# One score tile of two PSUM banks, with one maximum, scaling, sum and reciprocal per tile of tokens

## The chip, the core and the metric

One core of one Trainium2 chip. The metric is the device time of one execution in microseconds, lower is better. TensorE (PE) multiplies, VectorE (DVE) and ScalarE (ACT) work element by element, GpSimd (POOL) does one product per half tile, and SyncE (SP) issues all DMAs. Each engine runs its instructions in the order in which they stand in its queue.

## The reference

```python
def _attn_ref(q, k, v):                       # (4, 8, 576, 64): batch, heads, tokens, head size
    scores = scale * np.matmul(q, k.transpose(0, 1, 3, 2))
    rel = pos[:, None] - pos[None, :]
    scores = np.where((rel >= 0) & (rel < 64), scores, -1000000000.0)
    scores = scores - np.max(scores, axis=-1, keepdims=True)
    attn = np.exp(scores)
    attn = attn / (np.sum(attn, axis=-1, keepdims=True) + 1e-09)
    return np.matmul(attn, v)

def _moe_ref(x, w_in, w_out, g_ln):           # x (2304, 512), w_in (512, 1024), w_out (1024, 512)
    h = x @ w_in
    e = np.exp(h - np.max(h, axis=-1, keepdims=True))
    solu = h * (e / (np.sum(e, axis=-1, keepdims=True) + 1e-09))
    ln = (solu - mean(solu)) / np.sqrt(var(solu) + 1e-06) * g_ln
    return ln @ w_out

def _moe2_ref(x, w_in, w_out, a, b):          # w_in (512, 2048), w_out (2048, 512)
    h = x @ w_in
    g = (a[0] + a[1]*h + a[2]*h**2 + a[3]*h**3) / (1 + abs(b[0])*abs(h) + abs(b[1])*h**2 + 1e-06)
    return g @ w_out
```

The output is `_moe2_ref(_moe_ref(attention))` over 2304 tokens.

## The kernel before

The 2304 tokens are 18 tiles of 128. A first stage carries each tile through attention and the first expert layer; a second stage does the second expert layer in 6 blocks of 384 tokens. The weights come as 64-bit floats and are converted on the chip, chunk by chunk of 512 columns. The chunks are named `i` (first layer in, 8 half chunks), `o` (first layer out, 8) and `c` (second layer, 32). For each, ACT reads the words twice, DVE does a clamp (L518), a shift (L520), a merge (L522), an add (L525) and a remainder (L313 or L540), and ACT the rounded high part. A product of two 32-bit matrices is three products of high and low parts.

One tile t passes these steps; their names stand in `step(...)`:

- `scores` (L412, L418): PE adds the mask and multiplies q by k for 8 heads. The heads lie in two PSUM tiles of one bank each, `s{t}_0` and `s{t}_1`, four heads a tile.
- `max0`, `max1` (L426, L427): for each half, DVE takes the maximum per head and scales it.
- `exp00` to `exp13` (L432): ACT takes one exponential per head, with its sum.
- `sum0`, `sum1` (L438, L439): for each half, DVE adds 1e-9 and takes the reciprocal of four sums.
- `norm0`, `norm1` (L443): POOL multiplies a half by its reciprocals.
- `probs0`, `probs1` (L449): PE transposes a half; ACT copies it out (L317).
- `attend` (L466): PE multiplies by v. `att_hi`, `att_lo` (L317, L313): high part and remainder `xh`, `xl`.
- `h0` to `h3` (L554 to L556): 24 products into `h`, two PSUM banks, of which there is one pair (ring `h` of 1).
- `solu_max` (L562), `solu_exp` (L566), `solu_mul` (L571): maximum over 1024 columns, exponential, product. `solu_mul` gives `h` back, so that the next tile's `h0` can start.
- `ln_square` to `ln_apply` (L578 to L604): the layer norm. `lnT0`, `lnT1` (L614): transposes. `ln_hi`, `ln_lo`: high part and remainder.
- Every third tile: `x2_0` to `x2_3` (L632 to L634), the output products of three tiles, which need all `o` chunks.

The order is not written out by hand. The class `Schedule` gives each step a due time (from `WANT`, `PACE` and a table `SHIFT` of one number per step), then walks through time with a duration for each step and takes on each engine the ready step that is due first. `RINGS` says how many tiles of a kind may be held at once (scores: one tile of tokens). The names `L...` are lines of the profile.

Of the kernel before, what the change touches and what calls it, by code (L numbers as in the profile page):

```python
# [10 lines left out]
F32 = mybir.dt.float32  # L11
# [4 lines left out]
AF = mybir.ActivationFunctionType  # L16
ALU = mybir.AluOpType
AX = mybir.AxisListType
# [10 lines left out]
class Schedule:  # L29
# [248 lines left out]
def attention_moe_moe2(ctx: ExitStack, tc, q, k, v, w1, w1o, g_ln, w2, w2o, num, den, out):  # L278
# [122 lines left out]
    def scores(t):  # L401
# [18 lines left out]
        for j in range(2):  # L420
            tiles["s", t, j] = s[j]

    def soft_max(t, j):
        mx, su, rc = stat[t]
        sl = slice(NPAIR * j, NPAIR * j + NPAIR)
        nc.vector.reduce_max(mx[:, sl], tiles["s", t, j], axis=AX.X, negate=True)  # L426
        nc.vector.tensor_scalar_mul(mx[:, sl], mx[:, sl], 0.125)  # L427
# [611 lines left out]
```

## Time and profile before

| | |
|---|---|
| time, median of 3 runs | 728.79 us (728.03 to 729.09) |
| the profiled execution's own time | 727.53 us |
| its span, first to last instruction | 725.8 us |
| PE busy | 691.9 us (95%) |
| DVE busy | 615.3 us (85%) |
| ACT busy | 498.6 us (69%) |
| POOL busy | 48.0 us (7%) |
| mean granted clock of PE | 0.991 |

Busy time is the union of an engine's instructions. Successive instructions of one engine can overlap by some tenths of a microsecond, so the price of one in a row of them is read from start to start. The granted clock is a share of PE's full speed: 1.00 is 2.4 GHz, 0.50 is 1.2 GHz.

### The profile page before, as it was taken

What the parts mean: (1) busy time and instruction counts of PE and PEld (TensorE: products, weight loads), DVE (VectorE), ACT (ScalarE), POOL (GpSimd) and SP (SyncE); (2) the same over time, 40 slices, a digit from 0 to 9 for tenths busy, and PEclk for the clock granted to TensorE, in tenths of its full rate; (3) what the DMA queues carried; (4) which work ended last, traced back from release to release, by engine and by line L of the source; (5) the groups of instructions that cost most, each with busy time, mean ns of one, the idle gap of its engine ahead of it and who ended that gap; (6) DMA issues with size and microseconds to landing.
All of it is one profiled execution on the core that took longest, in us unless ns stands there. A gap on an engine that the chain in (4) does not pass through costs nothing.

```text
span 725.8 us, 12000 instructions
## 1 busy us (share of the span) xinstructions
PE 691.9 (95%) x4536; PEld 617.8 (85%) x4536; DVE 615.3 (85%) x999; ACT 498.6 (69%) x986; POOL 48.0 (7%) x51
## 2 busy tenths in 40 slices
PE   2689789999999999999999999999999999999997
PEld 1567579998988989999899999899899889899986
DVE  6999988989999997777999889688878778876873
ACT  6898775777677774657776766666665658566662
POOL 3212120012111110000000000000000000000000
PEclk9999989999999999999999999999999999999999
DMA  9764445667578635506220200010020001000001
GB/s 292 281 190 132 162 148 193 209 217 249 193 222 293 204 108 201 166 20 218 80 87 12 77 1 22 35 32 0 23 66 1 22 1 45 0 1 30 15 0 44
DMA packets 47785, 77.85 MB, mean 107 GB/s; under 512 B 5040, under 2 KB 23472, under 8 KB 47728
## 3 DMA queue, kind: packets, MB, share of 16 engines
q1 hardware_dynamic: 47728, 77.09, 32.7%
q8 instruction: 36, 0.59, 0.3%
q14 instruction: 21, 0.17, 0.1%
HBM read 59.25 MB, written 17.83 MB: 106 GB/s over the span
## 4 chain that ended last, share of the span: by engine, by line
PE 90%; DVE 4%; ACT 2%; DMA 2%; issue 1%; SPq 0%; POOL 0%; POOLq 0%
PE hp L829 9%; PE hp L828 9%; PE hp L827 9%; PE o L893 9%; PE o L892 9%; PE o L891 9%; PE x L632 5%; PE x L634 5%; PE x L633 5%; PE h L554 4%; PE h L555 4%; PE h L556 4%; PE pl L614 2%; PE s L418 2%; PE pv L466 2%; PE pt L449 2%
## 5 line engine op out<-in xcount | busy, mean ns | idle before, releaser
L829 PE MATMUL hp<-x2h,w 128*128 128x384 f32 x384 | 129.5, 337 | 0.0
L827 PE MATMUL hp<-x2h,w 128*128 128x384 f32 x384 | 129.3, 337 | 0.0
L828 PE MATMUL hp<-x2l,w 128*128 128x384 f32 x384 | 129.3, 337 | 0.0
L893 PE MATMUL o<-w,gl 128*128 128x512 f32 x282 | 111.4, 395 | 0.0
L892 PE MATMUL o<-w,gh 128*128 128x512 f32 x282 | 111.0, 394 | 0.0
L891 PE MATMUL o<-w,gh 128*128 128x512 f32 x282 | 110.8, 393 | 0.0
L837 ACT ACTIVATE w<-hp,ab 128x768 f32<-128x768 f32 x48 | 43.4, 905 | 72.6 <-PE hp L829 72.6
L845 DVE SCALAR_TENSOR_TENSOR w<-r,b,w 128x768 f32<-128x768 f32 x48 | 48.8, 1017 | 38.9 <-ACT r L839 38.9
L827 PEld LDWEIGHTS hp<-x2h,w 128*128 128x128 f32 x384 | 72.1, 188 | 3.2
L828 PEld LDWEIGHTS hp<-x2l,w 128*128 128x128 f32 x384 | 72.1, 188 | 3.2
L829 PEld LDWEIGHTS hp<-x2h,w 128*128 128x128 f32 x384 | 72.1, 188 | 0.3 <-DVE w L313 0.3
L875 ACT CAST gh<-t 128x768 fp32r<-128x768 f32 x48 | 40.3, 839 | 41.9 <-PE o L892 35.3
L632 PE MATMUL x<-lh,wo 128*128 128x384 f32 x192 | 66.7, 347 | 0.0
L554 PE MATMUL h<-wi,xh 128*128 128x512 f32 x144 | 58.9, 409 | 6.6 <-ACT xh L317 3.9
L634 PE MATMUL x<-lh,wo 128*128 128x384 f32 x192 | 65.0, 339 | 0.0
L633 PE MATMUL x<-ll,wo 128*128 128x384 f32 x192 | 65.0, 338 | 0.0
L893 PEld LDWEIGHTS o<-w,gl 128*128 128x128 f32 x282 | 52.9, 188 | 12.3
L892 PEld LDWEIGHTS o<-w,gh 128*128 128x128 f32 x282 | 52.9, 188 | 9.5
L891 PEld LDWEIGHTS o<-w,gh 128*128 128x128 f32 x282 | 52.9, 188 | 9.2
L443 POOL TENSOR_TENSOR P<-P,rc 128x512 f32<-128x512 f32 x36 | 44.8, 1248 | 224.9 <-DVE rc L439 127.7
L313 DVE TENSOR_TENSOR gl<-t,gh 128x768 fp32r<-128x768 f32 x48 | 45.9, 956 | 16.1 <-ACT gh L875 16.0
L556 PE MATMUL h<-wi,xl 128*128 128x512 f32 x144 | 57.1, 397 | 2.2 <-DVE xl L313 2.2
(105 smaller groups left out, 1495.1 us busy)
## 6 DMA issues: line engine op xcount, KB each, us to landing
v<-in_v_dram SPq DMA_DIRECT2D x35, 256.0 KB, 4.6
xc<-in_moe_w_in_dram SPq DMA_DIRECT2D x16, 512.0 KB, 3.6
w2d<-Ac SPq DMA_DIRECT2D x32, 256.0 KB, 3.2
xc<-in_moe_w_out_dram SPq DMA_DIRECT2D x16, 512.0 KB, 4.1
r<-w2d SPq DMA_DIRECT2D x32, 256.0 KB, 3.3
k<-in_k_dram SPq DMA_DIRECT2D x17, 384.0 KB, 4.8
q<-in_q_dram SPq DMA_DIRECT2D x18, 256.0 KB, 3.5
x2d<-xs SPq DMA_DIRECT2D x6, 768.0 KB, 4.5
```

The lines of the kernel that those rows point to most:

```text
L554: nc.tensor.matmul(o, xh[:, c, :], wh, start=(c == 0), stop=False)
L556: nc.tensor.matmul(o, xl[:, c, :], wh, start=False, stop=(c == KC - 1))
L632: nc.tensor.matmul(o, wh, lh[:, f, :], start=(f == 0), stop=False)
L633: nc.tensor.matmul(o, wh, ll[:, f, :], start=False, stop=False)
L634: nc.tensor.matmul(o, wl, lh[:, f, :], start=False, stop=(f == FC1 - 1))
L827: nc.tensor.matmul(h, wh[:, sl], xh[:, c], start=(c == 0), stop=False)
L828: nc.tensor.matmul(h, wh[:, sl], xl[:, c], start=False, stop=False)
L829: nc.tensor.matmul(h, wl[:, sl], xh[:, c], start=False, stop=(c == KC - 1))
L845: nc.vector.scalar_tensor_tensor(out=w, in0=r, scalar=b1, in1=w, op0=ALU.mult, op1=ALU.add)
L891: nc.tensor.matmul(o, gh[:, n, sl], wh, start=(f == 0), stop=False)
L892: nc.tensor.matmul(o, gh[:, n, sl], wl, start=False, stop=False)
L893: nc.tensor.matmul(o, gl[:, n, sl], wh, start=False, stop=(f == FC2 - 1))
```

## The change

The two score tiles become one tile `s{t}` over two banks. `max0` and `max1` become `max`, `sum0` and `sum1` become `sum`. The exponentials, the products on POOL and everything behind them stay as they were, except that each waits for the joint step. Some durations by which the planner reckons are edited, and the table `SHIFT` has new numbers for nearly all steps, so the order of all engines is another one. `WANT`, `PACE`, `ALT` and `RINGS` are the same. Behind the change, lines 410 to 440 stand 3 to 6 lines higher: L426 is then L421, L438 is L432, L562 is L556, L571 is L565.

```diff
@@ -167,106 +167,102 @@
 SHIFT = {
-    "zeros.0": 13.46, "load_q.0": 28.35, "load_k.0": 44.58, "load_v0.0": 54.08, "load_v1.0": 16.74, "scores.0": 14.59,
+    "zeros.0": -29.74, "load_q.0": 8.57, "load_k.0": -32.25, "load_v0.0": 110.71, "load_v1.0": 3.99, "scores.0": 4.78,
...
-    pS = psS.enter_context(tc.tile_pool(name="pS", bufs=2, space=PSUM, side="right"))
+    pS = psS.enter_context(tc.tile_pool(name="pS", bufs=1, space=PSUM, side="right"))
...
-        s = [pS.tile([P, NPAIR, P], F32, name=f"s{t}_{j}", tag="S") for j in range(2)]
+        both = pS.tile([P, 2, NPAIR, P], F32, name=f"s{t}", tag="S")
+        s = [both[:, j] for j in range(2)]
...
-        for j in range(2):
-            tiles["s", t, j] = s[j]
-
-    def soft_max(t, j):
+        tiles["s", t] = both
+
+    def soft_max(t):
         mx, su, rc = stat[t]
-        sl = slice(NPAIR * j, NPAIR * j + NPAIR)
-        nc.vector.reduce_max(mx[:, sl], tiles["s", t, j], axis=AX.X, negate=True)
-        nc.vector.tensor_scalar_mul(mx[:, sl], mx[:, sl], 0.125)
+        nc.vector.reduce_max(mx, tiles["s", t].rearrange("p j c k -> p (j c) k"), axis=AX.X, negate=True)
+        nc.vector.tensor_scalar_mul(mx, mx, 0.125)
...
-        nc.scalar.activation(Pn[t][:, j, n, :], tiles["s", t, j][:, n, :], AF.Exp, bias=mx[:, c:c + 1], scale=0.125,
+        nc.scalar.activation(Pn[t][:, j, n, :], tiles["s", t][:, j, n, :], AF.Exp, bias=mx[:, c:c + 1], scale=0.125,
                              accum_out=su[:, c:c + 1])
 
-    def soft_sum(t, j):
+    def soft_sum(t):
         mx, su, rc = stat[t]
-        sl = slice(NPAIR * j, NPAIR * j + NPAIR)
-        nc.vector.tensor_scalar_add(rc[:, sl], su[:, sl], 1.0e-9)
-        nc.vector.reciprocal(rc[:, sl], rc[:, sl])
+        nc.vector.tensor_scalar_add(rc, su, 1.0e-9)
+        nc.vector.reciprocal(rc, rc)
...
-        step("scores", "PE", 1.2, ["load_q", "load_k", ("constants", 0), ("zeros", 0)], scores, t, want=WANT["scores"],
+        step("scores", "PE", 1.25, ["load_q", "load_k", ("constants", 0), ("zeros", 0)], scores, t, want=WANT["scores"],
              take=[("s", t), ("P", t)], give=[("q", t), ("k", t)])
+        step("max", "DVE", 1.42, ["scores"], soft_max, t)
         for j in range(2):
-            step(f"max{j}", "DVE", 0.87, ["scores"], soft_max, t, j)
             for n in range(4):
-                step(f"exp{j}{n}", "ACT", 0.36, [f"max{j}"], soft_exp, t, j, n, give=[("s", t)])
-            step(f"sum{j}", "DVE", 0.35, [f"exp{j}{n}" for n in range(4)], soft_sum, t, j)
-            step(f"norm{j}", "POOL", 1.12, [f"sum{j}"], soft_norm, t, j)
+                step(f"exp{j}{n}", "ACT", 0.36, ["max"], soft_exp, t, j, n, give=[("s", t)])
+        step("sum", "DVE", 0.37, [f"exp{j}{n}" for j in range(2) for n in range(4)], soft_sum, t)
+        for j in range(2):
+            step(f"norm{j}", "POOL", 1.12, ["sum"], soft_norm, t, j)
...
-        step("attend", "PE", 0.98, ["probs_copy0", "probs_copy1", "load_v0", "load_v1"], attend, t, want=WANT["attend"],
+        step("attend", "PE", 1.05, ["probs_copy0", "probs_copy1", "load_v0", "load_v1"], attend, t, want=WANT["attend"],
...
-            step(f"h{c}", "PE", 1.385, needs + [("cv7", "i", c, hf) for hf in range(2)], h_mm, t, c,
+            step(f"h{c}", "PE", 1.39, needs + [("cv7", "i", c, hf) for hf in range(2)], h_mm, t, c,
...
-            step(f"lnT{hf}", "PE", 0.434, ["ln_apply"] + needs + ([("lnT1", t - 1)] if t else []), ln_T, t, hf,
+            step(f"lnT{hf}", "PE", 0.45, ["ln_apply"] + needs + ([("lnT1", t - 1)] if t else []), ln_T, t, hf,
...
-                step(f"x2_{dc}", "PE", 4.2, needs + [("cv7", "o", c) for c in range(FC1)], x2_mm, pr, dc,
+                step(f"x2_{dc}", "PE", 4.25, needs + [("cv7", "o", c) for c in range(FC1)], x2_mm, pr, dc,
```

Three places show how the order moves. In the rows below the number behind a tile's letters is the tile of tokens or the weight chunk (`rc6`: reciprocals of tile 6; `wo_7`: `o` chunk 7), the last number only counts buffers.

**First pair**: DVE ahead of the fifth `solu_mul` (`e4`). Before:

```order
L588 TENSOR_SCALAR st3_1064<-st3_1064 128x1
L540 SCALAR_TENSOR_TENSOR wo_7_1167<-Ao_7_873,gT_98,wo_7_1167 128x512
L562 TENSOR_REDUCE st4_1188<-h4_1127 128x1
L540 SCALAR_TENSOR_TENSOR wo_2_1181<-Ao_2_984,gT_98,wo_2_1181 128x512
L438 TENSOR_SCALAR rc6_899<-sum6_898 128x4
L439 RECIPROCAL rc6_899<-rc6_899 128x4
L518 TENSOR_SCALAR co_5_1151<-co_5_1151 128x512
L313 TENSOR_TENSOR ll0_794<-pl2_0_1067,lh0_793 128x4x128
L571 ISA e4_1189,st4_1188<-h4_1127,e4_1189 128x1024
```

The same place of DVE now:

```order
L534 SCALAR_TENSOR_TENSOR wo_2_1151<-Ao_2_848,gT_98,wo_2_1151 128x512
L556 TENSOR_REDUCE st4_1169<-h4_1102 128x1
L309 TENSOR_TENSOR ll0_670<-pl2_1_1144,lh0_669 128x4x128
L432 TENSOR_SCALAR rc7_1031<-sum7_1030 128x8
L433 RECIPROCAL rc7_1031<-rc7_1031 128x8
L516 SCALAR_TENSOR_TENSOR co_6_1008<-xo_6_831,co_6_1008 128x512
L565 ISA e4_1170,st4_1169<-h4_1102,e4_1170 128x1024
```

Between the maximum of tile 4 and its product stood the second half sum of tile 6; now the joint sum of tile 7 stands there, and that of tile 6 some 30 rows further up.

**Second pair**: PE at the first `h` product (tile 0). Before:

```order
L466 MATMUL pv0_295<-PT0_1_288,v0_1_204 64x64
L554 MATMUL h0_352<-wi_0_0_177,xh0_293 128x512
L555 MATMUL h0_352<-wi_0_0_177,xh0_293 128x512
L556 MATMUL h0_352<-wi_0_0_177,xl0_294 128x512
L554 MATMUL h0_352<-wi_0_1_229,xh0_293 128x512
L555 MATMUL h0_352<-wi_0_1_229,xh0_293 128x512
L556 MATMUL h0_352<-wi_0_1_229,xl0_294 128x512
L412 LDWEIGHTS ib_96
L412 MATMUL s2_0_374<-masks_97,ib_96 64x512
```

The same place of PE now:

```order
L415 MATMUL s2_358<-k2_265,q2_311 64x128 x16
L443 MATMUL pt1_1_397<-ident_95,P1_219 128x128 x4
L443 MATMUL pt1_0_408<-ident_95,P1_219 128x128 x4
L548 MATMUL h0_422<-wi_0_0_192,xh0_292 128x512
L549 MATMUL h0_422<-wi_0_0_192,xh0_292 128x512
L550 MATMUL h0_422<-wi_0_0_192,xl0_293 128x512
L548 MATMUL h0_422<-wi_0_1_256,xh0_292 128x512
```

The scores of tile 2 and both transposes of tile 1 stood behind the first step of `h`; now they stand ahead of it.

**Third pair**: DVE at `ln_newton` and `ln_apply` of tile 3 (`st3`, `e3`), which its `lnT0` waits for. Before:

```order
L520 TENSOR_SCALAR cc_8_1385<-cc_8_1385 128x512
L525 ISA Ac_2_1204<-cc_2_1203,rc_2_1205 128x1024
L522 SCALAR_TENSOR_TENSOR cc_8_1385<-xc_8_1292,cc_8_1385 128x512
L597 TENSOR_SCALAR st3_1064<-st3_1064 128x1
L598 TENSOR_SCALAR st3_1064<-st3_1064 128x1
L599 TENSOR_SCALAR st3_1064<-st3_1064 128x1
L525 ISA Ac_8_1386<-cc_8_1385,rc_8_1387 128x1024
L604 TENSOR_SCALAR e3_1065<-e3_1065,st3_1064 128x1024
```

The same place of DVE now:

```order
L534 SCALAR_TENSOR_TENSOR wo_5_1312<-Ao_5_1077,gT_98,wo_5_1312 128x512
L421 TENSOR_REDUCE mx9_1315<-s9_1318 128x8
L422 TENSOR_SCALAR mx9_1315<-mx9_1315 128x8
L516 SCALAR_TENSOR_TENSOR cc_0_1233<-xc_0_1128,cc_0_1233 128x512
L512 TENSOR_SCALAR cc_4_1345<-cc_4_1345 128x512
L309 TENSOR_TENSOR xl7_1350<-pv7_1351,xh7_1349 128x512
L519 ISA Ac_0_1234<-cc_0_1233,rc_0_1235 128x1024
L591 TENSOR_SCALAR st3_1017<-st3_1017 128x1
L592 TENSOR_SCALAR st3_1017<-st3_1017 128x1
L593 TENSOR_SCALAR st3_1017<-st3_1017 128x1
L514 TENSOR_SCALAR cc_4_1345<-cc_4_1345 128x512
L598 TENSOR_SCALAR e3_1018<-e3_1018,st3_1017 128x1024
```

The layer norm of tile 3 stood behind steps of `c` chunks 2 and 8; now it stands behind the last `o` chunk, the maximum of tile 9 and steps of `c` chunks 0 and 4. On PE, `lnT0` of tile 3 stood behind `x2_1`; now it stands behind `x2_0`.

## Rows read from the trace of the kernel before

**Rows 1.** Stretches: start:end length, busy us of each engine (instructions), PEclk, DMA share, GB/s.

```profile
20.00:40.00 20.00, 14.46 (x165) 10.89 (x158) 19.56 (x43) 16.99 (x53) 5.04 (x4) 0.84 0.64 220
...
80.00:100.00 20.00, 13.70 (x82) 10.35 (x81) 17.86 (x42) 16.55 (x55) 2.44 (x2) 0.83 0.51 162
100.00:120.00 20.00, 20.00 (x169) 18.91 (x168) 18.48 (x41) 13.14 (x26) 3.83 (x3) 1.00 0.68 210
...
700.00:720.00 20.00, 20.00 (x91) 16.69 (x91) 12.86 (x14) 8.63 (x11) 0.00 (x0) 1.00 0.00 1
```

**Rows 2.** Timeline of PE: start, duration, instruction, [idle before it <- releaser].

```profile
70.47 0.50 PE L554 MATMUL h<-wi,xh 128*128 128x512 f32 x1 [1.02 <-DVE st L571]
...
76.05 0.60 PE L449 MATMUL pt<-ident,P 128*128 128x128 f32 x4
76.58 0.41 PE L412 MATMUL s<-masks,ib 64*64 64x512 bf16 x4
...
77.79 0.66 PE L614 MATMUL pl<-ident,e 128*128 128x128 f32 x4
78.38 1.15 PE L466 MATMUL pv<-PT,v 128*64 128x64 f32 x32
...
88.83 0.60 PE L449 MATMUL pt<-ident,P 128*128 128x128 f32 x4
92.91 1.11 PE L449 MATMUL pt<-ident,P 128*128 128x128 f32 x4 [3.48 <-POOL P L443]
...
96.23 0.79 PE L554 MATMUL h<-wi,xh 128*128 128x512 f32 x1
...
102.91 0.60 PE L449 MATMUL pt<-ident,P 128*128 128x128 f32 x4
...
104.93 0.42 PE L632 MATMUL x<-lh,wo 128*128 128x384 f32 x1
...
109.26 0.60 PE L449 MATMUL pt<-ident,P 128*128 128x128 f32 x4
```

**Rows 3.** Timeline of DVE.

```profile
25.33 0.69 DVE L313 TENSOR_TENSOR xl<-pv,xh 128x512 fp32r<-128x512 f32 x1
...
41.20 1.22 DVE L562 TENSOR_REDUCE st<-h 128x1 f32<-128x1024 f32 x1 [0.24 <-PE h L556]
...
78.71 0.68 DVE L426 TENSOR_REDUCE mx<-s 128x4 f32<-128x512 f32 x1
...
79.50 0.68 DVE L525 CUSTOM_DVE_ANT_0 Ao<-co,ro 128x1024 uint16<-128x1024 uint16 x1
...
83.53 0.42 DVE L518 TENSOR_SCALAR co<-co 128x512 f32<-128x512 f32 x1
83.86 0.69 DVE L522 SCALAR_TENSOR_TENSOR co<-xo,co 128x512 uint32<-128x512 uint32 x1
84.46 0.42 DVE L520 TENSOR_SCALAR co<-co 128x512 uint32<-128x512 uint32 x1
...
91.27 0.16 DVE L438 TENSOR_SCALAR rc<-sum 128x4 f32<-128x4 f32 x1
...
91.56 0.40 DVE L518 TENSOR_SCALAR co<-co 128x512 f32<-128x512 f32 x1
...
92.48 1.21 DVE L571 CUSTOM_DVE_ANT_0 e<-h,e 128x1024 f32<-128x1024 f32 x1
...
96.35 0.69 DVE L426 TENSOR_REDUCE mx<-s 128x4 f32<-128x512 f32 x1 [1.49 <-PE s L418]
...
110.12 0.81 DVE L604 TENSOR_SCALAR e<-e,st 128x1024 f32<-128x1024 f32 x1
```

**Rows 4.** Groups by line: busy us, mean ns of one | idle before, releaser.

```profile
L562 DVE TENSOR_REDUCE st<-h 128x1 f32<-128x1024 f32 x18 | 21.9, 1219 | 5.7 <-PE h L556 5.6
```

**Rows 5.** Timelines of POOL and DVE around 45 us.

```profile
44.69 2.49 POOL L443 TENSOR_TENSOR P<-P,rc 128x512 f32<-128x512 f32 x2 [6.21 <-DVE rc L438]
45.02 1.26 DVE L518 TENSOR_SCALAR co<-co 128x512 f32<-128x512 f32 x1
```

More of the change, by code (lines that the diff above doesn't have):

```diff
@@ L169 @@
 SHIFT = {
[46 rows of a table removed]
-    "h3.s2": -2.93, "solu_max.s": 8.41, "solu_exp.s": 13.29, "solu_mul.s": -58.49, "ln_square.s": 12.49,
-    "ln_eps.s": -10.94, "ln_var.s": -0.24, "ln_root.s": -21.28, "ln_newton.s": -18.87, "ln_apply.s": 21.88,
[33 rows of a table removed]
-    "load_coefficients.s": 0.72, "coefficients.s": -6.98, "close_attention.s": -23.56, "close_conv.s": -11.88,
[17 rows of a table removed]
-    "o.s": 99.3, "oc.s": 37.1, "os.s": -30.11, "ol.s": 20.24,
[44 rows of a table added]
+    "solu_max.s": 24.36, "solu_exp.s": -51.68, "solu_mul.s": -123.49, "ln_square.s": -9.25, "ln_eps.s": -16.1,
+    "ln_var.s": -4.58, "ln_root.s": -78.69, "ln_newton.s": 6.74, "ln_apply.s": 0.09, "lnT0.s2": -43.18,
[31 rows of a table added]
+    "cv.c_31": 93.65, "load_coefficients.s": -1.46, "coefficients.s": -42.02, "close_attention.s": -8.96,
[17 rows of a table added]
+    "oc.s": -26.81, "os.s": 9.26, "ol.s": 26.47,
 }
```

186 rows, old and new, of the table SHIFT are left out of this document.

## The prediction, made before the changed kernel was run

> **What bounds the kernel now.** I read the stretches first [rows 1]. From 100 us to 720 us TensorE (PE) is busy in every microsecond (20.00 of 20 in all 31 stretches; the first and the last stand there) at a granted clock of 1.00. Nothing that another engine does there is waited for. What is not PE is ahead of 100 us: in 20 to 40 and 80 to 100 us PE is busy 14.46 and 13.70 of 20 and the clock falls to 0.84 and 0.83, while VectorE (DVE) is busy 19.56 and 17.86. So the end of the kernel is set by how much PE work is done by the time PE stops stopping, and I follow one point in both orders: the start of the first output product, x2_0 of tile 2 (L632), at 104.93 us [rows 2].
>
> The PE rows just before it [rows 2] show the last stop. At 88.83 PE transposes one half of tile 6's probabilities, then stands 3.48 us for GpSimd's (POOL's) product of the other half, and goes on at half clock: the same L449 group takes 1.11 us at 92.91 and 0.60 at 76.05; the h product of tile 5 takes 96.23 to 102.91 = 6.68 us, that of tile 3, 70.47 to 76.05 = 5.58. POOL was late because DVE was: the sum and reciprocal it waits for stand at 91.27 [rows 3], in the order behind two finished weight chunks and tile 4's L562 (first pair of order pieces). DVE in order is the bound of the ramp, and PE waits are its consequence.
>
> **The change, part by part.** Until the fifth L571 (tile 4's product, which frees the h banks for tile 5) DVE's old order holds 16 half maxima, 15 half sums and the rest; the new one holds 8 joint maxima, 8 joint sums, and of everything else the same plus three conversion steps of one more weight chunk.
> Prices, start to start [rows 3]: a half maximum with its scaling 79.50 - 78.71 = 0.79; a half sum with its reciprocal 91.56 - 91.27 = 0.29; a joint sum the same (its eight columns against four are nothing beside a fixed 0.29). A joint maximum reads 1024 columns of PSUM over two banks, as L562 does: 1219 ns [rows 4] against 0.68 for the half, so 0.79 + 0.54 = 1.33. The three conversion steps: 0.33 + 0.60 + 0.33 = 1.26 (83.53 to 83.86, 83.86 to 84.46, the third as the first).
> Before: 16 x 0.79 + 15 x 0.29 = 16.99. After: 8 x 1.33 + 8 x 0.29 + 1.26 = 14.22. DVE gets there 2.77 us sooner. The fifth L571 ends at 92.48 + 1.21 = 93.69 now, so at 90.92.
>
> Now PE. In the old order the half of tile 6 and the scores of tile 8 stood, late, between that end and h of tile 5, which so began 2.54 us after it could (96.23 against 93.69). In the new order tile 6's joint sum stands ahead of tile 3's L562, some 30 rows before the fifth L571, so its halves are long there so its halves are long there and h of tile 5 begins at 90.92. What PE has to do between h of tile 4 and this point (transposes, attend of tile 6, scores of tile 8, transposes: 3.4 us) lies beside tile 4's maximum, exponential and product, 1.22 and 1.21 on DVE and one like them on ACT, 3.6 us. It runs at full clock: 5.58, to 96.50. Then the new order has one transpose group (0.53, 76.05 to 76.58), scores of tile 9 (1.21, 76.58 to 77.79), the attend group of tile 7 (1.15 busy at 78.38) and one more transpose group (0.53): 3.42, and x2_0 at 99.92. Counting PE's steps ahead of x2_0 in both orders, the new one has done exactly one scores, one transpose group and one attend more: 1.21 + 0.53 + 1.15 = 2.89 us of work that it need not do later. The old kernel, with that added, would stand at 104.93 + 2.89 = 107.82. Gain 107.82 - 99.92 = **7.9 us**.
>
> Behind x2_0 the new order asks for tile 3's normalised rows (lnT0 of tile 3) after x2_0 (109.26 - 104.93 = 4.33) and a transpose group, at 99.92 + 4.33 + 0.53 = 104.8. DVE's way from the fifth L571 to tile 3's L604 is then nine two-input steps (0.60), five scalings (0.33), two joint maxima, one sum and 1.8 of small steps: 11.8 us, that is 102.7 if nothing holds it. In the old order the like stretch (eleven, seven, two half maxima, two sums, 1.8) counts 12.9 and took 110.93 - 93.69 = 17.2: 4.3 of waits, of which 1.49 is the wait at 96.35 for scores at half clock, gone in the new order. So 102.7 to 107.0; I take 102.7 + 4.3 - 1.5 = 105.5, the old stretch less what is known to go: a stop of 0.7 us. Net gain 7.2 us, against the profiled execution's own 727.53: 720.3. The median of the three runs is 1.26 above that execution, so on it 728.79 - 7.2 = **721.6 us**.
>
> Taken at nothing: the 5.4 us that the ten tiles behind save on DVE (0.25 in maxima and 0.29 in sums each) and the edited durations in the planner's steps, since PE waits for nobody after 100 us [rows 1]; the loads moved in SP's queue (the second tile's q and k ahead of two weight chunks), as DVE asks for the last of these chunks only behind its third maximum; the single score tile, so that the next tile's mask product waits for all eight exponentials and not four, since a whole h of 5.58 us lies between (were that cover gone, a stop as in rival two opens).
> Bounds on the sum: while POOL works, a DVE scaling can be held: at 45.02 one took 1.26 instead of 0.42, with POOL's two products from 44.69 for 2.49 [rows 5], 0.84 a hit. By PE's steps one more product lies ahead of x2_0 than before (17 against 16); if it hits, that costs 0.8, and four hits fewer would give 3.4. With the stop at lnT0 between 0 and 2.2, the forecast's own range is 717.5 to 724.
> The Trainium skill speaks here against the change (SBUF — State Buffer, Who interferes with whom): GpSimd and a VectorE scaling in a two-port mode exclude each other for a whole instruction. The change starts both products of a tile together, so that a scaling could be shut out for two products, 2.5 us. The rows [rows 5] have the hold: it ended inside the first of two back-to-back products' 2.49, so a hit is priced at one and not at two; priced at two, the one product more would cost 2.1 in place of 0.8.
>
> **The rivals.**
> One, *the first tile gives half of it back*. The new order puts tile 0's attended remainder (L313 xl, at 25.33 in the old trace) behind five conversion steps each of two more half chunks (2 x 2.46 = 4.9) and 0.8 of maxima and sums: done 26.0 + 5.7 = 31.7 instead of 26.0, and the new PE order starts no h before it (second pair of order pieces). Four h steps and one scores are 6.8 us at full clock, 13.6 at half: the first h ends at 38.5 to 45.3, against 41.0 (L562 at 41.20, 0.24 after PE [rows 3]). At the far end DVE stands 4.3 us at tile 0's L562, and all behind it moves: 721.6 + 4.3 = 725.9. For it: in [rows 1] the clock fell in this stretch already. Against: DVE reaches this L562 with the same work as before, and PE has 2.5 us in hand at full clock.
> Two, *slower: DVE comes too late behind x2_0*. If DVE reaches tile 3's L604 at 108.3 or later, 3 us beyond my sum, PE stands 3.5 us, as before 92.91, and goes on at half clock: 3.48 + 1.58 (the transposes and scores from 92.91 to 96.23 take 3.32 instead of 1.74) + 1.10 (h) = 6.2 us. One such stop leaves a gain of 1.7; from the second (the next tiles are asked in the same rhythm) the kernel is slower: 728.79 - 7.9 + 12.4 = 733.3. For it: in the new order lnT0 of tile 3 is asked right behind one x2 step while tile 3's last steps on DVE stand behind two weight chunks and one maximum (third pair of order pieces). Against: DVE has less to do per tile, and each later point that I counted has 3 us or more in hand.
> Three, *nothing*: the exponentials, copies and ln chains on ScalarE bound the ramp as much as DVE does, and what DVE saves turns into waits there: 728.8 within 1.4. For it: in the new order the sum waits for all eight exponentials, so POOL's first product starts later after the scores. Against: [rows 1] and the stop at 92.91, whose releaser is DVE's own order.
>
> **How the numbers follow.** Forecast 0.63, one 0.14, two 0.13, three 0.10. A measurement tells this kernel from no change at about 0.2%, 1.5 us. Faster by more: forecast, rival one and a little of three, 0.78. Within 0.2%: most of three, 0.07. Slower: two and the rest of three, 0.15. The range takes the forecast's own (717.5 to 724) and rival one's 725.9 with its neighbourhood, and leaves rival two and most of three out: 717 to 727.
>
> **What would show it.** Right: joint L421 (the old L426) near 1.22 us, half as many sums; the fifth e<-h,e product ending near 91 us; h of tile 5 within 0.3 us of it, with the clock at 1.00 from 60 us on; x2_0 near 100 us, no stop of PE over 1 us behind it. Wrong: tile 0's maximum over h (L562, then L556) beyond 43 us (rival one); a PE stop of over 3 us behind x2_0 with the clock at half again (rival two); the fifth product at 93.7 or later with ScalarE named as releaser (rival three). The sum itself would be wrong if PE's steps took another time over one score tile of two banks than over two tiles, which no row shows.

## The result: 721.2 us, and the profile after

The changed kernel takes 721.17 us in the median (720.6 to 721.7) against 728.83 us; the ratio is 0.9894, interval 0.9875 to 0.9914. One more execution of 1387 us, and one of 3866 us of early_exp_no_add below, are disturbed ones and are left out. The profiled execution took 720.6 us, its span is 718.8 us, PE is busy 688.4 us, DVE 602.5 us, ACT 495.1 us. The forecast was 721.6 us. The medians differ by 7.7 us and the two profiled executions by 6.9 (727.53 - 720.6), against the 7.2 of the forecast. The total is right, but the trace shows that four of the terms behind it are not, and that their errors nearly cancel: that it came so close is luck.

Stretches of the changed kernel, columns as in [rows 1]:

```profile
20.00:40.00 20.00, 13.10 (x138) 10.33 (x137) 19.01 (x37) 16.81 (x54) 4.54 (x4) 1.00 0.72 252
...
80.00:100.00 20.00, 18.68 (x206) 15.21 (x206) 18.40 (x41) 19.00 (x62) 3.10 (x3) 1.00 0.63 198
100.00:120.00 20.00, 20.00 (x152) 19.82 (x149) 19.72 (x41) 15.84 (x42) 4.15 (x4) 1.00 0.63 205
```

From 80 to 100 us PE is busy 18.68 of 20 at full clock, where it was 13.70 at 0.83 [rows 1]. The PE timeline there answers to [rows 2]:

```profile
92.26 0.66 PE L443 MATMUL pt<-ident,P 128*128 128x128 f32 x4 [0.22 <-POOL P L437]
92.67 0.48 PE L548 MATMUL h<-wi,xh 128*128 128x512 f32 x1
...
98.24 0.60 PE L443 MATMUL pt<-ident,P 128*128 128x128 f32 x4
98.77 0.41 PE L409 MATMUL s<-masks,ib 64*64 64x512 bf16 x4
...
99.98 1.15 PE L460 MATMUL pv<-PT,v 128*64 128x64 f32 x32
101.06 0.66 PE L443 MATMUL pt<-ident,P 128*128 128x128 f32 x4
101.47 0.42 PE L626 MATMUL x<-lh,wo 128*128 128x384 f32 x1
```

The stop of 3.48 us is 0.22, h of tile 5 runs at full clock (98.24 - 92.67 = 5.57), and x2_0 starts at 101.47 instead of 104.93. DVE's rows, as in [rows 3]:

```profile
40.97 1.21 DVE L556 TENSOR_REDUCE st<-h 128x1 f32<-128x1024 f32 x1
...
88.61 1.23 DVE L556 TENSOR_REDUCE st<-h 128x1 f32<-128x1024 f32 x1 [0.99 <-PE h L550]
...
91.22 1.22 DVE L565 CUSTOM_DVE_ANT_0 e<-h,e 128x1024 f32<-128x1024 f32 x1
...
105.12 0.81 DVE L598 TENSOR_SCALAR e<-e,st 128x1024 f32<-128x1024 f32 x1
```

The fifth product ends at 91.22 + 1.22 = 92.44, 1.25 us sooner than before, not 2.77. The last row shows no idle time of DVE ahead of tile 3's normalised rows, and PE does not stop for them; it transposes them here:

```profile
106.23 0.60 PE L608 MATMUL pl<-ident,e 128*128 128x128 f32 x4
```

Four starts on PE show where the time went: x2_0; the first product of the second expert layer (hp); the last output product of the first one (x); the last matmul. They are read from the timelines of the two kernels and, below, of the experiments:

| kernel | x2_0 | first hp | last x | last matmul | x2_0 to hp | last x to end |
|---|---|---|---|---|---|---|
| before | 104.93 | 301.60 | 327.68 | 721.64 | 196.67 | 393.96 |
| changed | 101.47 | 296.02 | 322.01 | 714.68 | 194.55 | 392.67 |

So 3.46 us came ahead of x2_0; 2.12 us between x2_0 and the first hp; 0.09 us up to the last x; and 1.29 us in the second expert layer, where the forecast had nothing. Together 6.96 us. The 2.12 are two things that the traces tell apart, start to start and by kind of product. PE has 2.96 us less to do there: one tile's scores (1.21), one transpose group (0.67) and one attend group (1.08) are done already. But the 112 transposes of normalised rows take 12.33 us instead of 11.68 and the 480 output products 86.72 instead of 86.53, 0.84 us more for the same work.

### The profile page after: what moved, and what is told of

Same layout as the page of the kernel before. It is cut to its first block, busy times and chain, and to the rows that moved or that the text cites. A ratio compares the mean times of both kernels' runs of the same rounds, so it can differ in the third digit from the quotient of the medians.

```text
span 718.8 us, 11925 instructions
## 1 busy us (share of the span) xinstructions
PE 688.4 (96%) x4536; PEld 617.4 (86%) x4536; DVE 602.5 (84%) x930; ACT 495.1 (69%) x983; POOL 46.3 (6%) x51
## 4 chain that ended last, share of the span: by engine, by line
PE 92%; ACT 4%; DVE 1%; DMA 1%; issue 1%; SPq 0%; POOL 0%; ACTq 0%
PE hp L824 9%; PE hp L822 9%; PE hp L823 9%; PE o L888 9%; PE o L887 9%; PE o L886 9%; PE x L626 5%; PE x L628 5%; PE x L627 5%; PE h L548 4%; PE h L550 4%; PE h L549 4%; PE pv L460 2%; PE s L415 2%; PE pl L608 2%; PE pt L443 2%
## 5 line engine op out<-in xcount | busy, mean ns | idle before, releaser
L548 PE MATMUL h<-wi,xh 128*128 128x512 f32 x144 | 58.2, 404 | 0.9 <-DVE st L565 0.9
L437 POOL TENSOR_TENSOR P<-P,rc 128x512 f32<-128x512 f32 x36 | 43.1, 1217 | 215.7 <-DVE rc L433 99.7
L549 PE MATMUL h<-wi,xh 128*128 128x512 f32 x144 | 56.4, 391 | 0.0
L427 ACT ACTIVATE P<-s,mx 128x128 f32<-128x128 f32 x144 | 51.5, 377 | 4.7 <-DVE mx L422 4.7
```

The costliest lines, as they stand in the source:

```text
L548: nc.tensor.matmul(o, xh[:, c, :], wh, start=(c == 0), stop=False)
L549: nc.tensor.matmul(o, xh[:, c, :], wl, start=False, stop=False)
```

## Experiments: is it the steps or the order?

The ramp is the stretch ahead of x2_0. Theory D is the prediction's: DVE, in order, bounds the ramp, so its saved time is gained one for one. Rival O: the new order makes the gain, and saved DVE time becomes waits. The first four kernels separate steps, order and tile.

**split_two_tiles**: new order, old steps and old tiles.

```
...
-        nc.vector.reduce_max(mx, tiles["s", t].rearrange("p j c k -> p (j c) k"), axis=AX.X, negate=True)
-        nc.vector.tensor_scalar_mul(mx, mx, 0.125)
+        for j in range(2):
+            sl = slice(NPAIR * j, NPAIR * j + NPAIR)
+            nc.vector.reduce_max(mx[:, sl], tiles["s", t][j], axis=AX.X, negate=True)
+            nc.vector.tensor_scalar_mul(mx[:, sl], mx[:, sl], 0.125)
...
-        nc.vector.tensor_scalar_add(rc, su, 1.0e-9)
-        nc.vector.reciprocal(rc, rc)
+        for j in range(2):
+            sl = slice(NPAIR * j, NPAIR * j + NPAIR)
+            nc.vector.tensor_scalar_add(rc[:, sl], su[:, sl], 1.0e-9)
+            nc.vector.reciprocal(rc[:, sl], rc[:, sl])
```

> The new order of all engines, but the old step code: two score tiles of one bank, and inside each max and sum step two half maxima, two scalings, two adds, two reciprocals. Theory D (DVE in order bounds the ramp): 8 maxima and 8 sums ahead of the fifth e<-h,e product cost 0.25 + 0.29 us more each, 4.3 us in all, so 721.2 + 4.3 = 725.5 us (724 to 726.5), and the fifth product ends near 96 us. Rival O (the new order alone makes the gain, and what DVE saves in the steps turns into its waits): 721.2 within 0.7, the fifth product near 92.5.

**split_one_tile**: the same steps over the one tile of two banks; against split_two_tiles:

```
...
-            nc.vector.reduce_max(mx[:, sl], tiles["s", t][j], axis=AX.X, negate=True)
+            nc.vector.reduce_max(mx[:, sl], tiles["s", t][:, j], axis=AX.X, negate=True)
```

> As the kernel with two tiles, but over the one score tile of two banks, so that the next scores wait for all eight exponentials. Theory D: the three waits of PE for exponentials (5.59, 5.32 and 3.37 us ahead of 50 us) lie ahead of a point that DVE sets, so the time is that of the kernel with two tiles within 0.7 us. Rival W (the single tile's wait delays the scores, and with them the chain): 1 to 3 us slower than with two tiles.

**old_order_joint_max**: the old order, its first half step joined, its second left empty, one tile.

```
...
+        if ("max", t) in tiles:
+            return
+        tiles["max", t] = True
+        nc.vector.reduce_max(mx, tiles["s", t].rearrange("p j c k -> p (j c) k"), axis=AX.X, negate=True)
+        nc.vector.tensor_scalar_mul(mx, mx, 0.125)
...
```

> The kernel before with its own order, one score tile, and one joint maximum with one scaling in the place of the first half's step (nothing in the second's); the sums stay halves. Theory D: 8 x 0.25 = 2.0 us of DVE less ahead of the fifth product: 728.8 - 2.0 = 726.8 (726 to 727.6). Rival O: 728.8 within 0.7. With rival W, slower than 728.8.

**old_order_one_tile**: the old order, half maxima and half sums, one tile. It was run later, to tell what made the kernel above slower.

```
-        s = [pS.tile([P, NPAIR, P], F32, name=f"s{t}_{j}", tag="S") for j in range(2)]
+        both = pS.tile([P, 2, NPAIR, P], F32, name=f"s{t}", tag="S")
+        s = [both[:, j] for j in range(2)]
...
```

> The kernel before with its order and its half steps, but over one score tile of two banks. The same order with one tile and a joint maximum was 1.9 us slower than before, where 2 us faster was expected. Theory W (the tile: the next scores wait for all eight exponentials of the tile before, and the old order has them in a place where that is late): 730.5, as there, or above. Rival J (the joint maximum: the first exponentials start 0.54 us later, and that is on the chain in the old order): 728.5 within 0.7.

| kernel | median | ratio to before, interval | x2_0 | last matmul |
|---|---|---|---|---|
| split_two_tiles | 722.35 | 0.9915 (0.9902 to 0.9929) | 102.95 | 716.35 |
| split_one_tile | 722.41 | 0.9919 (0.9905 to 0.9932) | 102.53 | 715.96 |
| old_order_joint_max | 730.51 | 1.0027 (1.0016 to 1.0037) | 107.31 | 724.16 |
| old_order_one_tile | 730.49 | 1.0027 (1.0017 to 1.0037) | 107.86 | 724.96 |

Neither D nor O holds. With the old steps the new order still gains 6.2 us (728.58 - 722.35); the joint steps are worth the rest, 0.9915 - 0.9894 = 0.0021 or 1.5 us, a third of the 4.3 us of DVE work that they save ahead of the fifth product. The two intervals overlap; the traces agree, with x2_0 at 102.95 against 101.47. The price of the steps was right: in the changed kernel the joint maximum starts at 21.05 and the row behind its scaling at 22.37, 1.32 us.

```profile
21.05 1.21 DVE L421 TENSOR_REDUCE mx<-s 128x8 f32<-128x1024 f32 x1
...
22.37 0.68 DVE L516 SCALAR_TENSOR_TENSOR ci<-xi,ci 128x512 uint32<-128x512 uint32 x1
```

The tile alone costs nothing in the new order (722.41 against 722.35), and 1.9 us in the old one, with half steps and with a joint maximum alike. So over one tile in the old order the joint maximum, with 2.0 us less of DVE work, gained nothing (730.51 against 730.49). Part of how the tile costs time there is seen in the first tile of old_order_one_tile; ACT's rows and DVE's:

```profile
11.49 0.37 ACT L432 ACTIVATE P<-s,mx 128x128 f32<-128x128 f32 x1
...
12.71 0.37 ACT L432 ACTIVATE P<-s,mx 128x128 f32<-128x128 f32 x1 [0.76 <-DVE mx L426]
```

```profile
11.98 0.69 DVE L426 TENSOR_REDUCE mx<-s 128x4 f32<-128x512 f32 x1
```

The second exponential starts when DVE's second half maximum ends (12.67). In the kernel before, with a tile for each half, it started at 11.83, while that maximum was running:

```profile
11.83 0.36 ACT L432 ACTIVATE P<-s,mx 128x128 f32<-128x128 f32 x1
```

```profile
11.88 0.68 DVE L426 TENSOR_REDUCE mx<-s 128x4 f32<-128x512 f32 x1
```

So in one tile the readers of different halves wait for each other in program order; the second exponential loses 0.9 us at the start of the ramp, and tile 0's first transposes on PE stand at 17.37 instead of 16.59. The Trainium skill (PSUM — Partial Sum Buffer, PSUM bank collisions raise a hardware error) asks for an order between two engines, two readers too, only on the same bank and 32 partitions; these two reads have a bank each, so the page does not ask for this wait; that the program keeps its dependencies by the tile is inferred from the traces: over all 18 tiles no exponential runs beside a half maximum in old_order_one_tile, and 27 do in the kernel before.

## Experiments: how far does DVE set the ramp?

**double_max**: DVE work added in tiles 0 to 7.

```
+        if t < 8:
+            nc.vector.reduce_max(mx, tiles["s", t].rearrange("p j c k -> p (j c) k"), axis=AX.X, negate=True)
```

> The changed kernel with the joint maximum of tiles 0 to 7 taken twice: 8 x 1.2 = 9.7 us more work on DVE ahead of the fifth e<-h,e product. Theory D (DVE in order is the bound, one for one): 721.2 + 9.7 = 730.9 (729.5 to 732). Rival S (the h banks' ring of product, maximum, exponential, product is as long as DVE's own work, so DVE has slack; 4.2 us more by the split steps cost 1.2 to 1.5): a third of it as there, 724.5, or, once some 3 us of slack are used up, the whole of the rest, 728.

**small_norm**: POOL's products over 8 of 128 columns. The kernel leaves out most of the normalisation.

```
-        nc.gpsimd.tensor_tensor(out=Pn[t][:, j], in0=Pn[t][:, j],
-                                in1=stat[t][2][:, sl].unsqueeze(2).broadcast_to([P, NPAIR, P]), op=ALU.mult)
+        nc.gpsimd.tensor_tensor(out=Pn[t][:, j, :, 0:8], in0=Pn[t][:, j, :, 0:8],
+                                in1=stat[t][2][:, sl].unsqueeze(2).broadcast_to([P, NPAIR, 8]), op=ALU.mult)
```

> The changed kernel with POOL's products over 8 of 128 columns, so that most of the normalisation is left out. It takes the holds of DVE by POOL away (ten of 0.4 to 0.9 us ahead of x2_0 in the changed kernel's trace, some 7 us) and up to 2 us of POOL per tile. Theory D: DVE is the bound, 7 us sooner: 714 (713 to 716). Rival S (DVE has slack, the h ring bounds): a third of that, 719 (718 to 720.5). If no hold reached the end: 721.2.

**split_late**: half steps from tile 9 on.

```
+        if t < 9:
+            nc.vector.reduce_max(mx, tiles["s", t].rearrange("p j c k -> p (j c) k"), axis=AX.X, negate=True)
+            nc.vector.tensor_scalar_mul(mx, mx, 0.125)
+        else:
+            for j in range(2):
...
```

> The changed kernel with half maxima and half sums for tiles 9 to 17 only. Theory D: PE waits for nobody behind 100 us, so the 9 x 0.54 = 4.9 us more on DVE cost nothing: 721.2 within 0.7. Rival L (part of the gain was made behind 100 us): up to 4.9 us slower, 726.

double_max took 728.62 us (its runs spread from 726.8 to 730.1), ratio 1.0002 (0.9991 to 1.0013), x2_0 at 110.80 in an execution of 729.9. Against the changed kernel's 0.9894 that is 7.9 us for 9.7 us of work. small_norm took 719.78 us, 0.9879 (0.9866 to 0.9892), 1.1 us less than the changed kernel's ratio gives, with intervals that overlap, and its x2_0 stands at 101.42, as in the changed kernel. Its DVE is busy 69.00 us from 10 to 90 us, that of the changed kernel 74.44. split_late took 720.7 us, 0.9891 (0.9878 to 0.9905): 4.9 us of DVE work behind 100 us cost nothing, as was taken.

So DVE in the new order has some slack, an estimate of 2 to 3 us by the medians (9.7 - 7.9 = 1.8; from the split, 4.3 - 1.5 = 2.8). The one trace of double_max (729.9 us) has x2_0 9.3 us later, which would leave 0.4, so the size is loose. Work beyond it costs about one for one (from split_two_tiles to double_max 5.4 us more work, 6.4 us more time), work taken away gains next to nothing. What takes over is PE; small_norm's rows on PE and then on DVE:

```profile
45.64 0.64 PE L409 MATMUL s<-masks,ib 64*64 64x512 bf16 x4 [3.08 <-ACT P L427]
46.02 1.97 PE L415 MATMUL s<-k,q 64*64 64x128 f32 x32
47.92 0.79 PE L548 MATMUL h<-wi,xh 128*128 128x512 f32 x1
```

```profile
55.48 1.23 DVE L556 TENSOR_REDUCE st<-h 128x1 f32<-128x1024 f32 x1 [3.38 <-PE h L550]
```

DVE stands 3.38 us for h of tile 1, which PE started late and at half clock, because the scores of tile 4 ahead of it waited for tile 3's last exponential (granted clock 0.50 from 45.6 to 48 us).

DVE's waits from 10 us to the end of the fifth product say the same of the changed kernel. Before, then after (us in total, times, longest):

```profile
DVE mx L426 <- PE s L418: 0.7, 2, 0.5
DVE st L562 <- PE h L556: 0.6, 2, 0.3
DVE xl L313 <- ACT xh L317: 0.4, 1, 0.4
DVE st L588 <- ACT sq L578: 0.3, 1, 0.3
```

```profile
DVE st L556 <- PE h L550: 2.1, 3, 1.0
DVE rc L432 <- ACT P L427: 0.5, 1, 0.5
DVE mx L421 <- PE s L415: 0.5, 2, 0.3
DVE wi L309 <- ACT wi L525: 0.4, 1, 0.4
DVE ci L512 <- ACT ci L507: 0.4, 1, 0.4
DVE rc L432 <- ACT st L586: 0.3, 1, 0.3
DVE st L582 <- ACT sq L572: 0.3, 1, 0.3
DVE e L565 <- ACT e L560: 0.2, 1, 0.2
```

And DVE's work in the same stretch (columns as in [rows 1], DVE the fourth figure), before and after:

```profile
10.00:93.69 83.69, 61.35 (x655) 47.40 (x648) 80.08 (x182) 71.85 (x222) 18.76 (x15) 0.95 0.61 205
```

```profile
10.00:92.44 82.44, 63.52 (x722) 51.30 (x718) 76.85 (x154) 72.63 (x224) 17.84 (x16) 0.98 0.64 210
```

DVE is busy 80.08 - 76.85 = 3.23 us less, and gets there only 1.25 us sooner: 3.23 - 1.25 = 1.98 us of the saved work came back as idle time. The waits listed grew by more, from 2.0 to 4.7 us, since short gaps without a releaser shrank; more than half of that growth is for PE's h.

## Experiments: what was behind PE's last stop?

**before_early_sum**: the kernel before; one half sum of tile 6 and its product moved up.

```
...
+        for key in ("norm1", 6), ("sum1", 6):
+            self.order.insert(place.index(("sum0", 6)) + 1, self.order.pop(place.index(key)))
...
```

> The kernel before, in which two steps alone are moved: the second half sum of tile 6 (at 91.27 us on DVE) and its product on POOL stand right behind the first half sum of tile 6, some 25 steps sooner; all eight exponentials of the tile are ahead of both places. Theory P (the last stop of PE came from this sum's place in DVE's order and nothing else): the 3.48 us wait at 92.91 goes, h of tile 5 begins when the fifth e<-h,e product ends, 93.7 instead of 96.23, at full clock (5.6 instead of 6.7): x2_0 3.6 us sooner, 101.3, and the kernel 728.5 - 3.6 = 724.9 us (724 to 726). Rival Q (another wait takes its place, for the fifth product or an attended tile): within 0.7 of 728.5.

It took 727.64 us, 0.9983 (0.9973 to 0.9992), with x2_0 at 103.20: 1.2 us of the 3.6. The stop is still there, but with another releaser:

```profile
92.48 1.12 PE L453 MATMUL pt<-ident,P 128*128 128x128 f32 x4 [2.94 <-DVE ll L317]
```

PE's second transpose group needs one of two PSUM banks, which it shares with the transposes of the normalised rows. The other holds the transposed rows of tile 2, and DVE reads these last (ll, 91.74 to 92.43 in this run). Before, the same step stands just ahead of the fifth product (L313 ll0 in the first pair of order pieces), and was hidden: POOL's product released PE 0.43 us later (92.91 against 92.48).

**before_early_two**: that step moved up as well.

```
...
+        for key, behind in ((("norm1", 6), ("sum0", 6)), (("sum1", 6), ("sum0", 6)), (("ln_lo0", 2), ("sum0", 7))):
+            self.order.insert(place.index(behind) + 1, self.order.pop(place.index(key)))
...
```

> As the kernel before with tile 6's second half sum and product moved up, and one DVE step more: the first remainder of tile 2's normalised rows (ll, at 91.74 us there), which gives back the PSUM bank that PE's second transpose group waited for until 92.48 in that run, stands right behind tile 7's first half sum (85.5). Theory P2 (PE's last stop had two causes 0.4 us apart, both of them places in DVE's order): h of tile 5 begins when the fifth e<-h,e product ends, 93.1 to 93.7, at full clock, x2_0 at 100.7 to 101.3, and the kernel 3.6 to 4.2 us faster than before: 724.4 to 725. Rival Q2 (a third wait stands right behind): as with the first move alone, 727.6.

It took 725.02 us, 0.9953 (0.9939 to 0.9967), x2_0 at 101.81. PE's rows:

```profile
90.17 1.03 PE L453 MATMUL pt<-ident,P 128*128 128x128 f32 x8
91.13 0.41 PE L416 MATMUL s<-masks,ib 64*64 64x512 bf16 x4
...
94.24 0.47 PE L558 MATMUL h<-wi,xh 128*128 128x512 f32 x1 [1.82 <-DVE st L575]
```

Both groups run back to back, and h waits for the product of DVE alone. Two moved steps give 3.1 us at x2_0. The whole new order with the old steps gives 104.93 + 2.12 - 102.95 = 4.1 there, so three quarters of the order's gain in the ramp is this one stop, as the prediction had it, but with two causes and not one.

## Experiments: the 1.3 us in the second expert layer

That layer has 96 chunks of hp products and 96 of o products. The new order changes 89 times between the two kinds, the old one 147 times.

**quads** (first) and **alternate** (second): the planner gets needs for PE's chunks alone (`g`: hp, `o`: o), the ramp stays as it is.

```
...
+    for i in range(16, NB2 * FC2, 4):
+        plan.extra["g", i] = [("o", i - 5)]
+        plan.extra["o", i - 4] = [("g", i + 3)]
```

```
...
+    for i in range(16, NB2 * FC2):
+        plan.extra["g", i] = [("o", i - 6)]
+        plan.extra["o", i - 5] = [("g", i)]
```

> The changed kernel, its order of the ramp untouched; in the second expert layer, from its 17th chunk on, PE takes four hp chunks, then four o chunks, and so on: 51 changes between hp and o products where the changed kernel has 89 and the kernel before 147. Theory C (behind x2_0 the changed kernel's PE took 1.4 us less than its moved work explains because it changes 58 times less between hp and o, 24 ns a change): 38 changes less, 0.9 us, so 720.3 (719.6 to 720.8). Rival R (the products' rate differs for another reason, or the two runs merely differ): 721.2 within 0.4, or slower if four chunks in a row wait for DVE.

> The same place the other way: one hp chunk, one o chunk in turn, 171 changes. Theory C: 82 changes more than in the changed kernel, 2.0 us, so 723.2 (722.4 to 723.8). Rival R: 721.2 within 0.4.

quads took 720.38 us, 0.9894 (0.9881 to 0.9907), as the changed kernel; alternate 729.98 us, 1.0018 (1.0009 to 1.0027), 9 us more. By the traces:

| kernel | changes | mean pitch of hp, o (ns) | last x to end | of it stops | without them |
|---|---|---|---|---|---|
| quads | 51 | 174.52, 230.67 | 392.78 | 0.62 | 392.16 |
| changed | 89 | 174.55, 231.20 | 392.67 | 0 | 392.67 |
| before | 147 | 175.08, 232.10 | 393.96 | 0 | 393.96 |
| alternate | 171 | 175.16, 232.18 | 402.40 | 8.30 | 394.10 |

The pitch is the time from start to start of two products of one kind; pitches over 260 ns are left out of it, and what those of o take beyond the mean is the column of stops. Without the stops the stretch grows with the number of changes over all four, but not evenly: 13, 22 and 6 ns a change from row to row. The 0.9 us that theory C gave quads did not come as time. So it is shown that the size of the 1.3 us goes with the order of the products; that it goes by the number of changes is not. Two things theory C did not foresee. The time is not lost at the changes: the pitch is longer all through both kinds (an hp product right behind a change takes 174.7 ns before and 175.7 after, the others 175.1 and 174.5). And alternate stops PE at each of the five changes of token block, since its first o product there comes one chunk behind the last of the block before and waits for the copies out of the three banks (the first of these stops stands below); two more, at 719 and 720 us, are for ScalarE and DVE:

```profile
396.15 0.50 PE L887 MATMUL o<-w,gh 128*128 128x512 f32 x1 [1.66 <-ACT os L314]
```

Four chunks in a row leave time for that copy, and so do the pairs of the changed kernel.

## Experiment: both limits at once

ACT takes six exponentials of tile 3 in a row and two later, and PE's scores of tile 4 wait for the last. In the changed kernel, ACT and then PE:

```profile
41.63 0.38 ACT L427 ACTIVATE P<-s,mx 128x128 f32<-128x128 f32 x1
...
45.53 0.41 ACT L427 ACTIVATE P<-s,mx 128x128 f32<-128x128 f32 x1
```

```profile
46.08 0.64 PE L409 MATMUL s<-masks,ib 64*64 64x512 bf16 x4 [3.37 <-ACT P L427]
46.46 1.97 PE L415 MATMUL s<-k,q 64*64 64x128 f32 x32
48.36 0.79 PE L548 MATMUL h<-wi,xh 128*128 128x512 f32 x1
```

**early_exp_no_add** moves these two forward on ACT and takes one step from DVE in every tile.

```
...
+        for key in ("exp01", 3), ("exp12", 3):
+            self.order.insert(place.index(("exp10", 3)) + 1, self.order.pop(place.index(key)))
...
-        nc.vector.tensor_scalar_add(rc, su, 1.0e-9)
-        nc.vector.reciprocal(rc, rc)
+        nc.vector.reciprocal(rc, su)
```

> The changed kernel with two edits: the last two exponentials of tile 3 stand right behind its first six on ACT (now 2 to 4 us later, and the scores of tile 4 wait for them 3.37 us, then run at half clock), and 1e-9 is not added to the sums (which are 1 or more), one DVE step less per tile. Theory T (two limits of the same length up to 55 us: DVE in order reaches tile 1's maximum over h at 54.06, PE ends that h at 54.41; either alone gives 0.5 at most): both together 1.0 to 1.4 us, x2_0 at 100.0 to 100.4 in place of 101.0 to 101.5, time 719.9. Rival: one of them is behind a third limit, x2_0 and time as in the changed kernel.

It leaves out the 1e-9, beside sums of 1 or more. It took 718.8 us, 0.9864 (0.9849 to 0.9879), the fastest of all: 0.9894 - 0.9864 = 0.0030 or 2.2 us less than the changed kernel, with intervals that just meet. x2_0 stands at 98.99, 2.48 us sooner than in the changed kernel's trace, and all of it reaches the end (last matmul 712.20 against 714.68). The scores of tile 4 now follow the transposes at once, and h of tile 1 waits for DVE only:

```profile
41.24 0.41 PE L413 MATMUL s<-masks,ib 64*64 64x512 bf16 x4
41.47 1.05 PE L419 MATMUL s<-k,q 64*64 64x128 f32 x32
45.37 0.48 PE L551 MATMUL h<-wi,xh 128*128 128x512 f32 x1 [2.85 <-DVE st L568]
```

More was gained than the 1.0 to 1.4 expected. Up to 0.9 us of the 2.48 is the scatter of single executions: the scores of tile 1, ahead of both edits, start at 15.13 instead of 16.01. Against the traces of quads and alternate, whose ramp is that of the changed kernel, x2_0 is 1.95 and 1.72 sooner. That taking 5.4 us of work from DVE alone (small_norm) gained 1.1 us, inside the intervals, and one small step a tile together with earlier exponentials twice that, is what two limits of one length would show. The two edits were not run apart: that the earlier exponentials alone make the gain is a rival that no run excludes.

## Why the prediction was right, and where its steps were not

The forecast was right in its total and in the way PE's last stop goes. Its first term and the worth of the moved work were too large by 2.3 us together, and two errors the other way, 2.0 us, made up for it.

| step | predicted | measured |
|---|---|---|
| joint maximum with scaling | 1.33 | 1.32 |
| fifth product ends | 90.92 | 92.44 |
| h of tile 5 | 5.58, from 90.92 | 5.57, from 92.67 |
| from there to x2_0 | 3.42 | 3.23 |
| x2_0 | 99.92 | 101.47 |
| work that PE has done ahead of it | 2.89 | 2.12 (2.96 less 0.84) |
| gain at x2_0 | 7.9 | 5.6 |
| stop at lnT0 of tile 3 | -0.7 | 0 |
| second expert layer | 0 | 1.3 |
| sum | 7.2 | 7.0 with 0.1 in between |

**The term that was mis-sized** is DVE's 2.77 us at the fifth product: 1.25 came. The count of work was right (3.23 us less busy); that all of it would reach the path was the fault. [Rows 1] had DVE at 17.86 to 19.56 of 20, and the text read this as a bound. It was one of two of nearly equal length: PE's h products with their wait for scores are the other, and from 50 to 100 us the changed PE idles for some 3 us only.

**PE's order** was read rightly: h of tile 5 at once, at full clock, and the transposes, scores and attend behind it in 3.23 us. The cause was half told: the product of POOL was the last to come by 0.43 us only, and DVE's late ll stood next to it in the same piece of order. The new order moves both, so the forecast did not suffer.

**The moved work** was counted rightly: 2.89 in starts, 2.96 by the traces. What the term lacked is that the order also changes the time of the products that stay: behind x2_0 the transposes of normalised rows take 0.65 us more and the output products 0.19, and 2.12 is left.

**The stop at lnT0** did not come: DVE ended that step at 105.93, 0.4 later than the sum, but PE asked for it at 106.2, 1.4 later than forecast. Two late things met.

**What was taken at nothing**: the steps of the later tiles are nothing (split_late). The order of the second layer is 1.3 us; the text looked at waits behind 100 us, found none, and did not look at the products' rate. For the single score tile the cover named, a whole h, is not there in the first tiles: the scores of tiles 1, 2 and 4 wait 5.59, 5.32 and 3.37 us for exponentials. Over two tiles of one bank, in split_two_tiles, they wait 5.12, 4.84 and 1.34 us, and the time is the same (722.35 against 722.41 over one): the single tile cost nothing by itself.

**The rivals.** One did not come: tile 0's maximum over h is at 40.97. Two did not: no stop of PE behind x2_0. Three, *nothing*, was closer than its 0.10: its mechanism, DVE's savings that turn into waits, took 1.52 of the 2.77 of the first term.

**POOL's holds** are there as bounded, and cost less than the range allowed. In the changed kernel POOL's two products of tile 3 take 47.38 to 50.11, and meanwhile a pair of L519 takes 2.08 (1.28 elsewhere) and then one L512 takes 1.14 (0.42): two instructions of DVE held by 0.8 and 0.7, none by two products. This agrees with the Trainium skill (SBUF — State Buffer, Who interferes with whom) in that an instruction is held whole. It bears out the prediction's price of one product a hit, here 0.7 to 0.8 us.

```profile
47.38 2.73 POOL L437 TENSOR_TENSOR P<-P,rc 128x512 f32<-128x512 f32 x2 [7.63 <-DVE rc L433]
```

```profile
47.13 2.08 DVE L519 CUSTOM_DVE_ANT_0 Ao<-co,ro 128x1024 uint16<-128x1024 uint16 x2
...
49.26 1.14 DVE L512 TENSOR_SCALAR co<-co 128x512 f32<-128x512 f32 x1
```

## What to carry to other kernels

A nearly full engine in the ramp is a bound only as long as the next chain is shorter; before its savings are counted one for one, look for that chain's slack in the same rows. Behind a stop with a named releaser, look for the step that would have released it next: here it was 0.43 us behind, and removing the named one alone gave 1.2 us of the 3.6 that were expected. An order can also change the time of an engine that never waits, so compare rates and not only waits.

## What was not expected of the hardware

PE's pitch in full stretches without a wait depends on how two kinds of products are interleaved: from 174.52 and 230.67 ns (51 changes) to 175.16 and 232.18 ns (171). In the seven kernels that have the changed order there it is 174.55 to 174.58 and 231.20 to 231.22, and in the five with the old order 175.04 to 175.08 and 232.07 to 232.10. The mechanism is open.

A stop of the same length does not always find the same clock behind it. Before, h of tile 4 starts after 2.83 us of idle time with a product of 0.50 us, and the granted clock from 83 to 86 us is 1.00; in before_early_two it starts after 2.82 us with one of 0.80, and the clock there is 0.50, the lower level. x2_0 scatters by up to 0.8 us between kernels whose ramp is the same (101.47 changed, 100.94 quads, 100.71 alternate), so a single trace does not settle less than that.
